# A gated mix of linear attention and a squared-ReLU layer: the first key-value burst queued as one block, and the first w1 tile loaded in four pieces

## The chip, the cores and the metric

The kernel runs on one core of one Trainium2 chip. The metric is the device time of one execution in microseconds (us); of several executions of one kernel the median counts.

## What is computed

The token matrix `x` (2048 x 512) goes through two branches, and a gate of one number per token mixes them. The input `B_x` is not used; both branches read `A_x`.

```python
g = sigmoid((x * gate_w).sum(-1, keepdims=True))
# branch a: 32 heads of 16, feature map with two softmaxes, linear attention
q, k, v = split(x @ wqkv)
phi(t)  = concat(softmax(t @ w_phi), softmax(-(t @ w_phi)))      # per head, 16 -> 32
kv, z   = phi(k)^T @ v, sum over tokens of phi(k)
a       = ((phi(q) @ kv) / (phi(q) . z + 1e-6)) @ wo
# branch b: dense layer of width 1792
h       = relu(x @ w1 + b1) ** 2
b       = h @ w2 + b2
out     = g * a + (1 - g) * b
```

## The kernel before, in words

**The dense layer paces everything.** The tokens are cut into 4 blocks of 512, the 1792 hidden columns into 14 tiles of 128. Two sweeps go over the 4 blocks, the first with hidden tiles 0 to 6, the second with 7 to 13, which makes 56 steps `t`. A step has an *up* product (`up`, tile `u`: 12 matmuls of 128 x 512) for step `t + 2` and the *down* products (`down`, tiles `d`: 4 token chunks of 3 matmuls each) for step `t`. Every fp32 product is written as three products of high and low parts (`mm3`, lines 73 to 77: high by high, line 75; high by low, line 76 or 77; low by high). The parts come from `split` (lines 65 to 71): ScalarE copies the high part (line 67), VectorE subtracts it to get the low part (line 70). `hidden` makes ReLU (line 455), square (456) and the split into `hh` and `hl`, which have three buffers each.

**The attention's work is laid between the steps.** Half of each step is a *slot*; `at(slot, f)` puts a function into a slot, and the loop at line 753 runs the functions of slot `2t`, the up product, the functions of slot `2t + 1`, then the down products. Keys and values are computed by pairs of token chunks with seven block products instead of eight (functions `p1` to `p7`, PSUM tiles `kx`, `ky`, `kz`); `features` turns a key chunk into exponentials, `normed` scales them, `values` writes a value chunk into `vext`. `do_kv(p)` then multiplies the features of pair `p` with its values: 64 matmuls of 32 columns (two chunks of 32, line 374), which all add into one PSUM tile `kvps` and which VectorE adds to `kvs` (line 612). This is the *key-value burst*; there are 8, one for each pair. Pair 1 begins at slot 13.5, so the first burst, of pair 0, is called in slot 17, ahead of the down products of step 8, together with `p7(1)` and `p3(1)`; `p4(1)` follows in slot 18. Slots 14, 16, 18 and 20 also load rows of `x` for the gate (`gate_load`, tile `in`), and two slots later VectorE multiplies and sums them (`gate_dot`, line 320).

**What sets the order.** The Tile scheduler orders each engine's instructions by priority and data. `tc.issue_after(i)` keeps what is written under it behind instruction `i` in the order; `tc.high_priority` pulls forward. After step 9's first two chunks of down products, `fold("q")` (line 202) builds a folded query weight: it fills two `u` tiles and both banks that `kx`, `ky` and `kz` use, and four VectorE transposes (line 224) empty them; the next up product and the next `kx` product need those banks again.

**The start.** `warm_up` runs 12 matmuls on constants. `start` (line 494) issues the four pieces of `x` on SP's queue (line 500), the first w1 tile on ScalarE's queue (line 501), then on SP two more w1 tiles and a w2 tile (`fetch`, line 109), then others. The first up product multiplies the raw fp32 pieces (line 518, for k = 0 to 3, each using columns `k * 128` to `k * 128 + 127` of the w1 tile). The next one (lines 469 and 471) needs the split parts of all four `x` pieces and of the second w1 tile; its first 128 columns are copied on their own (line 526).

The transfers of the two queues (SP's and ScalarE's) take turns on eight completion semaphores, named DMAHW0 to DMAHW7 in the program: a transfer waits until the one that had its semaphore before has landed.

Of the kernel before, what the change touches and what calls it, by code (L numbers as in the profile page):

```python
# [16 lines left out]
P = 128  # L17
S, D, H, DH, F = 2048, 512, 32, 16, 1792
NK = D // P
# [8 lines left out]
NV = 2  # L28
# [9 lines left out]
def tile_gated_mix(ctx: ExitStack, tc: tile.TileContext, xT, xn, wqT, wkT, wphi, wv, wo, w1, b1, w2, b2, gw, out):  # L38
    nc = tc.nc
# [14 lines left out]
    st, up_w, down_w = {}, {}, {}  # L54
# [10 lines left out]
    def split(src, hi, lo, ehi, elo):  # L65
        if ehi is nc.scalar:
            i = nc.scalar.activation(hi, src, AF.Copy)  # L67
        else:
            i = ehi.tensor_copy(hi, src)
        st["low"] = elo.tensor_tensor(lo, src, hi.bitcast(F32), ALU.subtract)  # L70
        return i
# [22 lines left out]
    def ffn_tiles(nm, fc):  # L94
        if fc >= NFH + NSTR:
            return slots(("B21", "T1", "T4", "T3")[fc - NFH - NSTR], int(nm == "w2"), f"{nm}{fc}")
        return (fpool.tile([P, 512], F32R, tag=nm + "h", name=f"{nm}h{fc}"),
                fpool.tile([P, 512], F32R, tag=nm + "l", name=f"{nm}l{fc}"))
# [5 lines left out]
    def fetch(nm, fc, t=None):  # L104
        src = w1[fc] if nm == "w1" else w2[fc * P:(fc + 1) * P, :]
        if t is None:
            t = load(src)
        else:
            nc.sync.dma_start(t, src)
        raw[nm, fc] = t  # L110
# [15 lines left out]
    def ready(nm, fc, elo=nc.vector):  # L126
        hi, lo = ffn_tiles(nm, fc)
        i = split(raw.pop((nm, fc)), hi, lo, nc.scalar, elo)
        (up_w if nm == "w1" else down_w)[fc] = hi, lo
        return i  # L130

    def ready_later(nm, fc, *elo):
        with tc.issue_after(st["act"].ins):
            ready(nm, fc, *elo)

    def x_tiles(b, k):
        return (xpool.tile([P, SB], F32R, tag="xh", name=f"xh{b}_{k}"),
                xpool.tile([P, SB], F32R, tag="xl", name=f"xl{b}_{k}"))
# [49 lines left out]
    vext = [hold.tile([P, H * VW + 32 - VW], F32, tag="vz", name=f"vext{i}") for i in range(NV)]  # L188
# [8 lines left out]
    def load_fold(nm, wT, tiles):  # L197
        st["wT", nm] = tiles
        for g in range(NK):
            nc.sync.dma_start(tiles[g], wT[:, g, :])  # L200
# [169 lines left out]
    def kv_chunk(n, kvps, phi, v):  # L370
        for i in range(NG):
            for j in range(4):
                h = 8 * (i % 4) + 4 * (i // 4) + j
                nc.tensor.matmul(kvps[32 * j:32 * j + 32, 32 * i:32 * i + 32], v[:, h * VW:h * VW + 32],  # L374
                                 phi[:, 32 * h:32 * h + 32],
                                 start=(n % 2 == 0 and i == 0), stop=(n % 2 == 1),
                                 skip_group_check=True)
# [75 lines left out]
    def hidden(fc, ps):  # L453
        r = work.tile([P, SB], F32, tag="r", name="r")
        nc.scalar.activation(r, ps, AF.Relu, bias=b1c[:, fc:fc + 1])  # L455
        nc.scalar.activation(r, r, AF.Square)  # L456
        hh = work.tile([P, SB], F32R, tag="hh", name="hh", bufs=LAG + 1)
        hl = work.tile([P, SB], F32R, tag="hl", name="hl", bufs=LAG + 1)
        st["act"] = split(r, hh, hl, nc.scalar, nc.vector)
        return hh, hl  # L460
# [33 lines left out]
    def start():  # L494
        w = work.tile([P, 2, 4, NG, 32], F32, tag="phiT", name="win", bufs=1).rearrange("p u r g s -> p (u r g s)")
        t = st["xr", 0] = [work.tile([P, 2 * D], F32, tag="tb", name="xin", bufs=2) for _ in range(2)]
        raw["w1", 0] = w[:, :D]
        xs = [t[k // 2][:, k % 2 * D:(k % 2 + 1) * D] for k in range(NK)]
        for k in range(NK):
            nc.sync.dma_start(xs[k], xT[0, :, k, :])  # L500
        nc.scalar.dma_start(w[:, :D], w1[0])
        fetch("w1", 1, w[:, D:2 * D])
        fetch("w1", 2, w[:, 2 * D:3 * D])
        fetch("w2", 0, w[:, 3 * D:])
        fetch("w1", 3)
        fetch("w2", 1)
        t = [wpool.tile([P, 512], F32, tag=tag, name="fold") for tag in ("T40h", "T30h", "T30l", "T31h", "T31l")]
        st["wphi"] = t[0]
        nc.sync.dma_start(t[0], wphi)
        load_fold("k", wkT, t[1:])  # L510
        fetch("w1", 4)
        fetch("w2", 2)
        ps = ps_u.tile([P, SB], F32, tag="u", name="u")
        st["x", 0] = []
        for k in range(NK):
            kk = slice(k * P, (k + 1) * P)
            with tc.issue_after(st["up"].ins):
                st["up"] = nc.tensor.matmul(ps, raw["w1", 0][:, kk], xs[k], start=k == 0, stop=k == NK - 1)
            hi, lo = x_tiles(0, k)
            split(xs[k], hi, lo, nc.scalar, nc.vector)  # L520
            st["x", 0].append((hi, lo))

        t = raw.pop(("w1", 1))
        hi, lo = up_w[1] = ffn_tiles("w1", 1)
        for j in (slice(0, P), slice(P, 512)):
            nc.scalar.activation(hi[:, j], t[:, j], AF.Copy)
        nc.vector.tensor_tensor(lo, t, hi.bitcast(F32), ALU.subtract)
        i = ready("w1", 2)
        with tc.issue_after(i.ins):
            hid[0] = hidden(0, ps)  # L530
        ready_later("w2", 0)
        with tc.issue_after(st["up"].ins):
            do_up(1)
        raw.pop(("w1", 0))
        fetch_v()
# [70 lines left out]

    def do_kv(p):
        ps = ps_u.tile([P, 2 * P], F32, tag="u", name="kvps")
        for m in (2 * p, 2 * p + 1):
            kv_chunk(m, ps, st["phi", m], vext[m % NV])  # L610
        with tc.high_priority(offset=AHEAD):
            nc.vector.tensor_tensor(kvs, kvs, ps, ALU.add)

# [48 lines left out]
    def at(slot, f, *a):  # L662
        steps.setdefault(int(slot), []).append(lambda: f(*a))
# [9 lines left out]
    for t in range(NB * NFH):  # L673
        for nm, s in (("w1", 2 * t - 8), ("w2", 2 * t - 4)):
            late = (nm, t % NFH) in KEPT_LATE
# [18 lines left out]
    at(20, foldq_move)  # L694
    starts = (8, 13.5, 20, 25.2, 30.4, 35.6, 40.8, 46)
    for p, s in enumerate(starts):
        todo = [(p1, s, p), (p6, s + 1, p), (p2, s + 1, p), (p5, s + 3, p)]
        if p:
            todo.append((do_kv, s + 3 + (p == 1), p - 1))
        todo += [(p7, s + 3 + (p == 1), p), (p3, s + 4, p), (p4, s + 5, p)]  # L700
        for f, slot, q in todo:
            at(slot, f, q)
    at(NB * SL - 2, do_kv, NPAIR - 1)
    for b in range(NB):
        for c in range(NC):
            s = b * SL + 2 * c if b else 7 + c
# [21 lines left out]
    for p in range(NB * NC // 2):  # L728
        n, s = 2 * p, 54 + 6 * p + 2 * (p > 0)
        q, late = divmod(n, NC)[0], p == NB * NC // 2 - 1  # L730
# [13 lines left out]
    def do_up(t):  # L744
        if t < len(work_list):
            sw, b, i = work_list[t]
            fc = sw * NFH + i
            hid[t] = up(fc, st["x", sw * NB + b], up_w[fc])
# [112 lines left out]
```

## Time and profile before

| | us |
|---|---|
| runs before, median of 3 (lowest, highest) | 510.41 (509.11, 511.47) |
| the profiled execution's own time | 508.94 |
| its span, from first to last instruction | 507.2 |
| matmul busy time on TensorE (PE) in the span | 503.0 |
| VectorE (DVE) / ScalarE (ACT) / GpSimd (POOL) busy | 404.0 / 254.2 / 75.0 |
| granted TensorE clock, mean | 0.999 of full |

A row of a timeline gives start, duration, engine, source line, operation, output and inputs, shape and count; in brackets stands how long the engine was idle before it and what ended that. Rows that repeat are merged, with the count behind the x. SPq and ACTq are the queues that issue transfers; PEld is the weight load that goes ahead of a matmul. A fp32 pass of a matmul counts as one instruction, and a 32-column matmul of the burst has two passes, so that a burst of 64 shows 128. A matmul's duration in a row is longer than its pitch, since matmuls overlap: what the next one waits is read from start to start.

### The profile page before, as it was taken

Reading aid. Unit: us, or ns where it says so; the run is one execution under the profiler, and the core shown is the slowest. Engines: PE = TensorE matmul, PEld = TensorE weight load, DVE = VectorE, ACT = ScalarE, POOL = GpSimd, SP = SyncE. Lnnn points to the kernel's source line nnn. Section 1 sums busy time; section 2 is a strip of 40 time slices with the busy share of each in tenths; the row PEclk is TensorE's granted clock in tenths of the full one; section 3 lists DMA queues with packets and bytes.
Section 4 is the critical chain, followed back from the end, with each engine's and each line's share of the span. In section 5 each row is a group of like instructions: output and inputs, shape, how many; then the busy total and the mean of one; then the engine's idle time right before and its main releaser. Section 6 shows DMA issues by size and latency. Waiting matters only on the chain.

```text
span 507.2 us, 9515 instructions
## 1 busy us (share of the span) xinstructions
PE 503.0 (99%) x3616; PEld 403.9 (80%) x3616; DVE 404.0 (80%) x642; ACT 254.2 (50%) x433; POOL 75.0 (15%) x77
## 2 busy tenths in 40 slices
PE   9999999999999999999999999999999999999997
PEld 4878877788888888888888878788787878788876
DVE  4979997867878777787889998978789676798724
ACT  6598571654654557273664744343525353433530
POOL 5303020202050000000004131202121212102100
PEclk9999999999999999999999999999999999999999
DMA  8899787984567656835658252213152221032102
GB/s 295 316 351 321 226 278 249 312 305 153 176 200 236 238 172 209 291 118 174 186 162 308 72 192 53 90 51 95 38 183 95 82 80 45 7 101 81 41 23 83
DMA packets 52437, 84.79 MB, mean 167 GB/s; under 512 B 8104, under 2 KB 14504, under 8 KB 52392
## 3 DMA queue, kind: packets, MB, share of 16 engines
q1 hardware_dynamic: 52072, 83.79, 51.1%
q8 instruction: 28, 0.46, 0.4%
q10 hardware_dynamic: 288, 0.39, 0.2%
q14 instruction: 17, 0.14, 0.1%
q0 software_dynamic: 32, 0.01, 0.0%
HBM read 56.37 MB, written 21.50 MB: 154 GB/s over the span
## 4 chain that ended last, share of the span: by engine, by line
PE 98%; ACT 1%; DVE 0%; issue 0%
PE d L75 10%; PE u L75 10%; PE d L77 10%; PE d L76 10%; PE u L76 10%; PE u L77 9%; PE q L75 3%; PE q L76 3%; PE q L77 3%; PE att L76 3%; PE att L77 3%; PE att L75 3%; PE ky L75 2%; PE ky L77 2%; PE ky L76 2%; PE kvps L374 2%
## 5 line engine op out<-in xcount | busy, mean ns | idle before, releaser
L455 ACT ACTIVATE r<-u,b1c 128x512 f32<-128x512 f32 x56 | 38.4, 686 | 148.8 <-PE u L77 148.8
L383 POOL TENSOR_TENSOR ez<-e,z 128x512 f32<-128x512 f32 x32 | 41.7, 1325 | 277.9 <-ACT e L354 160.5
L75 PE MATMUL d<-w2h,hh 128*128 128x512 f32 x160 | 63.1, 394 | 0.0
L77 PE MATMUL d<-w2h,hl 128*128 128x512 f32 x160 | 62.3, 390 | 0.0
L76 PE MATMUL d<-w2l,hh 128*128 128x512 f32 x160 | 62.3, 389 | 0.0
L75 PE MATMUL u<-xh,w1h 128*128 128x512 f32 x152 | 59.7, 393 | 0.1
L76 PE MATMUL u<-xl,w1h 128*128 128x512 f32 x152 | 59.2, 389 | 0.0
L77 PE MATMUL u<-xh,w1l 128*128 128x512 f32 x152 | 59.2, 389 | 0.0
L359 DVE TENSOR_REDUCE sm<-e 128x64 f32<-128x1024 f32 x32 | 38.9, 1214 | 20.3 <-ACT e L354 20.3
L70 DVE TENSOR_TENSOR hl<-r,hh 128x512 fp32r<-128x512 f32 x56 | 38.0, 678 | 16.0 <-ACT hh L67 16.0
L407 ACT ACTIVATE phiT<-tb 32x256 f32<-32x256 f32 x64 | 26.5, 413 | 32.1 <-DVE tb L401 31.5
L354 ACT ACTIVATE e<-e 128x1024 f32<-128x1024 f32 x32 | 33.8, 1055 | 12.6 <-DVE e L352 12.3
L67 ACT ACTIVATE hh<-r 128x512 fp32r<-128x512 f32 x56 | 35.3, 630 | 2.3 <-PE d L76 0.8
L456 ACT ACTIVATE r<-r 128x512 f32<-128x512 f32 x56 | 35.2, 629 | 1.3
L75 PEld LDWEIGHTS d<-w2h,hh 128*128 128x128 f32 x160 | 30.0, 188 | 6.5 <-issue 0.4
L272 POOL TENSOR_TENSOR row<-xin 128x256 f32<-128x256 f32 x16 | 17.8, 1120 | 117.4 <-DVE S4ol L70 27.6
L77 PEld LDWEIGHTS d<-w2h,hl 128*128 128x128 f32 x160 | 30.0, 188 | 6.3
L76 PEld LDWEIGHTS d<-w2l,hh 128*128 128x128 f32 x160 | 30.0, 188 | 6.0
L75 PEld LDWEIGHTS u<-xh,w1h 128*128 128x128 f32 x152 | 28.5, 188 | 7.9 <-issue 0.8
L77 PEld LDWEIGHTS u<-xh,w1l 128*128 128x128 f32 x152 | 28.5, 188 | 6.1
L76 PEld LDWEIGHTS u<-xl,w1h 128*128 128x128 f32 x152 | 28.5, 188 | 5.8
L385 DVE TENSOR_REDUCE dz<-ez 128x64 f32<-128x1024 f32 x16 | 19.4, 1210 | 9.4 <-POOL ez L383 9.3
(544 smaller groups left out, 1161.5 us busy)
## 6 DMA issues: line engine op xcount, KB each, us to landing
in<-in_w SPq DMA_DIRECT2D x66, 256.0 KB, 3.2
phiT<-tb SPq DMA_DIRECT2D x192, 32.0 KB, 1.9
w2l<-lkept SPq DMA_DIRECT2D x20, 256.0 KB, 4.0
w1l<-lkept SPq DMA_DIRECT2D x19, 256.0 KB, 3.5
xin<-in_xT SPq DMA_DIRECT2D x16, 256.0 KB, 5.7
xkept<-xh SPq DMA_DIRECT2D x16, 256.0 KB, 3.7
xkept<-xl SPq DMA_DIRECT2D x16, 256.0 KB, 4.2
in<-in_xn SPq DMA_DIRECT2D x16, 256.0 KB, 2.9
```

What stands on the lines that cost most here:

```text
L67: i = nc.scalar.activation(hi, src, AF.Copy)
L70: st["low"] = elo.tensor_tensor(lo, src, hi.bitcast(F32), ALU.subtract)
L75: nc.tensor.matmul(o, ah[:, sa], bh[:, sb], start=first, stop=False, **kw)
L76: nc.tensor.matmul(o, ah[:, sa], bl[:, sb], start=False, stop=False, **kw)
L77: return nc.tensor.matmul(o, al[:, sa], bh[:, sb], start=False, stop=last, **kw)
L354: nc.scalar.activation(ef, ef, AF.Exp)
L359: nc.vector.tensor_reduce(sm, e3, AX.X, ALU.add)
L383: nc.gpsimd.tensor_tensor(ez[:, hs, :], e3[:, hs, :], zbc[half], ALU.mult)
L385: nc.vector.tensor_reduce(dz, ez, AX.X, ALU.add)
L407: nc.scalar.activation(dst, src, AF.Copy)
L455: nc.scalar.activation(r, ps, AF.Relu, bias=b1c[:, fc:fc + 1])
L456: nc.scalar.activation(r, r, AF.Square)
```

## The change

In `do_kv`, the 64 matmuls stand under `tc.issue_after(st["down"].ins)`, that is, behind the last down product written so far. The first burst, `p7(1)` and `p3(1)` move from slot 17 to slot 18 (`late`). The first w1 tile is loaded on ScalarE's queue in four transfers of 128 columns (64 KB each, 512 bytes in each of 128 partitions) instead of one of 512 columns (256 KB, 2 KB in each).

```diff
-        nc.scalar.dma_start(w[:, :D], w1[0])
+        for k in range(NK):
+            kk = slice(k * P, (k + 1) * P)
+            nc.scalar.dma_start(w[:, kk], w1[0, :, kk])
...
     def do_kv(p):
         ps = ps_u.tile([P, 2 * P], F32, tag="u", name="kvps")
-        for m in (2 * p, 2 * p + 1):
-            kv_chunk(m, ps, st["phi", m], vext[m % NV])
+        with tc.issue_after(st["down"].ins):
+            for m in (2 * p, 2 * p + 1):
+                kv_chunk(m, ps, st["phi", m], vext[m % NV])
...
     for p, s in enumerate(starts):
+        late = 1.5 * (p == 1)
         todo = [(p1, s, p), (p6, s + 1, p), (p2, s + 1, p), (p5, s + 3, p)]
         if p:
-            todo.append((do_kv, s + 3 + (p == 1), p - 1))
-        todo += [(p7, s + 3 + (p == 1), p), (p3, s + 4, p), (p4, s + 5, p)]
+            todo.append((do_kv, s + 3 + late, p - 1))
+        todo += [(p7, s + 3 + late, p), (p3, s + 4 + late / 2, p), (p4, s + 5, p)]
```

On TensorE the order changes only around the first burst; the other seven bursts already stood as whole blocks and stay where they are. Before, right behind the up product of step 10, the burst's first matmuls stand between the down products of step 7 (`d_960` to `d_963` are its four chunks), and the other 58 follow behind them, ahead of `ky`, `kz` and the down products of step 8:

```order
L76 MATMUL u<-xl_3_606,w1h_780 128x512
L77 MATMUL u<-xh_3_605,w1l_781 128x512
L374 MATMUL kvps<-e,vext_114 32x32 x2
L75 MATMUL d_960<-w2h_768,hh 128x512
L76 MATMUL d_960<-w2l_769,hh 128x512
L77 MATMUL d_960<-w2h_768,hl 128x512
L374 MATMUL kvps<-e,vext_114 32x32 x2
L75 MATMUL d_961<-w2h_768,hh 128x512
L76 MATMUL d_961<-w2l_769,hh 128x512
L77 MATMUL d_961<-w2h_768,hl 128x512
L374 MATMUL kvps<-e,vext_114 32x32
L75 MATMUL d_962<-w2h_768,hh 128x512
```

Now the down products of steps 7 and 8 stand in one piece behind the up product (one `ky` matmul ahead of them), and this is the end of step 8's (`d_966`, its last chunk), where the burst follows as one block and the rest of `ky` and `kz` behind it:

```order
L75 MATMUL d_966<-w2h_777,hh 128x512
L76 MATMUL d_966<-w2l_778,hh 128x512
L77 MATMUL d_966<-w2h_777,hl 128x512
L374 MATMUL kvps<-e,vext_114 32x32 x32
L374 MATMUL kvps<-e,vext_115 32x32 x32
L76 MATMUL ky<-T30l,S_731 128x512
L77 MATMUL ky<-T30h,S_731 128x512
L75 MATMUL ky<-T31h,S_731 128x512
L76 MATMUL ky<-T31l,S_731 128x512
L77 MATMUL ky<-T31h,S_731 128x512
```

The burst has moved behind 24 down matmuls, and the five places where TensorE went to 32-column matmuls and back have become one. On VectorE, at the same place in the program (`hl` are low parts of the hidden tile, `in,lg` is the gate's product and sum, `vext` the values of pair 1, `k` the keys of its second chunk), the order was:

```order
L70 TENSOR_TENSOR hl<-r,hh 128x512
L612 TENSOR_TENSOR kvs<-kvs,kvps 128x256
L361 RECIPROCAL r<-sm 128x64
L320 SCALAR_TENSOR_TENSOR in,lg<-in,gwb 128x512
L365 TENSOR_TENSOR e<-e,r 128x1024
L564 TENSOR_TENSOR vext_115<-ky,t_1005 128x32x16
L564 TENSOR_TENSOR vext_114<-kz,t_900 128x32x16
L70 TENSOR_TENSOR hl<-r,hh 128x512
L320 SCALAR_TENSOR_TENSOR in,lg<-in,gwb 128x512
L564 TENSOR_TENSOR k_1149<-ky,t_847 128x512
L349 TENSOR_REDUCE mx<-k_1149 128x32
```

and is now:

```order
L70 TENSOR_TENSOR hl<-r,hh 128x512
L361 RECIPROCAL r<-sm 128x64
L320 SCALAR_TENSOR_TENSOR in,lg<-in,gwb 128x512
L365 TENSOR_TENSOR e<-e,r 128x1024
L70 TENSOR_TENSOR hl<-r,hh 128x512
L615 TENSOR_TENSOR kvs<-kvs,kvps 128x256
L566 TENSOR_TENSOR vext_115<-ky,t_1008 128x32x16
L320 SCALAR_TENSOR_TENSOR in,lg<-in,gwb 128x512
L566 TENSOR_TENSOR vext_114<-kz,t_903 128x32x16
L566 TENSOR_TENSOR k_1152<-ky,t_850 128x512
L349 TENSOR_REDUCE mx<-k_1152 128x32
```

The addition to `kvs` has moved behind the second `hl`, and the `vext` write from `kz` behind the second gate product. On SP's queue at the start (the waits in brackets are the completion semaphores), before:

```order
L500 DMA xin<-in_xT 128x512 x4
L109 DMA win<-in_w 128x512 x3
L85 DMA in<-in_w 128x512 [waits DMAHW0_49]
L85 DMA in<-in_w 128x512 [waits DMAHW1_49]
L509 DMA fold<-in_wphi 128x512 [waits DMAHW2_49]
L200 DMA fold<-in_wkT 128x512 [waits DMAHW3_49]
```

and now:

```order
L500 DMA xin<-in_xT 128x512 x4
L109 DMA win<-in_w 128x512 [waits DMAHW0_49]
L109 DMA win<-in_w 128x512 [waits DMAHW1_49]
L109 DMA win<-in_w 128x512 [waits DMAHW2_49]
L85 DMA in<-in_w 128x512 [waits DMAHW3_49]
L85 DMA in<-in_w 128x512 [waits DMAHW4_49]
L511 DMA fold<-in_wphi 128x512 [waits DMAHW5_49]
```

The four pieces of `x` and the four pieces of the first w1 tile now hold all eight semaphores, so that SP's fifth transfer, the second w1 tile, waits for the first piece of `x` to land; before, the first wait was in its eighth transfer. On ScalarE only the four transfers in place of one are new, and nothing moves on GpSimd.

## The prediction

> **What bounds the kernel now.** I read the page's busy times and its chain of waits first, then the timeline of TensorE around the first burst, at the fold that follows it, and at the start.
>
> ```profile
> PE 503.0 (99%) x3616; PEld 403.9 (80%) x3616; DVE 404.0 (80%) x642; ACT 254.2 (50%) x433; POOL 75.0 (15%) x77
> PE 98%; ACT 1%; DVE 0%; issue 0%
> ```
>
> TensorE is busy for 503.0 of 507.2 us, and 98% of the chain that ended last is TensorE. So time is won only where TensorE itself does less or waits less, and it is lost wherever TensorE is made to wait. The profiled execution took 508.94 us; the median of the runs is 510.41, 1.47 more. I work against the first and add the sum to both. About 0.5% (2.5 us) is what a measurement of this kernel can tell from no change; that is the bound of "faster" and "slower" below.
>
> **The burst: what it removes.** In the timeline of TensorE, each row with its start:
>
> ```profile
> 72.89 0.39 PE L77 MATMUL u<-xh,w1l 128*128 128x512 f32 x1
> 73.20 0.26 PE L374 MATMUL kvps<-e,vext 128*32 128x32 f32 x4
> ...
> 76.94 0.39 PE L76 MATMUL d<-w2l,hh 128*128 128x512 f32 x1
> ...
> 77.50 1.20 PE L374 MATMUL kvps<-e,vext 128*32 128x32 f32 x116
> ...
> 78.96 0.40 PE L76 MATMUL ky<-T30l,S 128*128 128x512 f32 x1
> ...
> 84.19 0.39 PE L75 MATMUL ky<-T40h,xh 128*128 128x512 f32 x1
> ...
> 106.91 0.39 PE L77 MATMUL kz<-T11h,S2ol 128*128 128x512 f32 x1
> 107.23 1.30 PE L374 MATMUL kvps<-e,vext 128*32 128x32 f32 x128
> ...
> 108.79 0.40 PE L76 MATMUL ky<-T30l,S2oh 128*128 128x512 f32 x1
> ```
>
> The pitch of an ordinary matmul comes from 78.96 to 84.19: 23 matmuls in 5.23 us, 0.227 us each. From 72.89 to 78.96 stand 14 ordinary matmuls (the last of the up product, 12 down, one `ky`), 14 x 0.227 = 3.18 us. The other 2.89 us went to the first burst and its five visits to 32-column matmuls. The second burst stands in one piece: from 106.91 to 108.79 are 1.88 us, less two matmuls (0.45) leaves 1.43. One piece instead of five saves 2.89 - 1.43 = **1.46 us** of TensorE's own time. No instruction is added or removed.
>
> Moved products could wait for data, but I find no such wait. The four chunks of step 7 need their banks emptied by VectorE, and the first would now start at about 73.35, the fourth at 75.39; these evacuations (line 806) stand back to back from 72.17 to 74.89, each half a microsecond ahead. If that cover went, the lost time would come off the 1.46.
>
> **The burst: what is late next.** TensorE reaches the fold 1.46 us earlier, and there it already waits for VectorE:
>
> ```profile
> 92.36 2.50 DVE L224 STREAM_TRANSPOSE wqin<-foldq 128x512 f32<-128x512 f32 x4
> ...
> 92.81 0.40 PE L77 MATMUL d<-w2h,hl 128*128 128x512 f32 x1
> ...
> 94.31 0.50 PE L75 MATMUL kx<-B110h,xh 128*128 128x512 f32 x1
> 94.65 0.40 PE L76 MATMUL kx<-B110l,xh 128*128 128x512 f32 x1
> ```
>
> From 92.81 to 94.65 are six pitches, 1.36 us, but 1.84 passed: TensorE lost 0.48 us, because `kx` needs the bank that the third of the four transposes empties (92.36 plus three quarters of 2.50 is 94.24). So there is no slack: whatever of the 1.46 us the transposes don't also move is lost again here. What the transposes wait for, in the order of time on SP's queue, VectorE and ScalarE:
>
> ```profile
> 77.37 0.32 SPq L118 DMA_DIRECT2D w2l<-lkept  x1
> ...
> 79.65 0.42 SPq L85 DMA_DIRECT2D in<-in_xn  x1
> ```
>
> ```profile
> 81.86 0.68 DVE L564 TENSOR_TENSOR vext<-kz,t 128x512 f32<-128x512 f32 x1
> 82.45 0.68 DVE L70 TENSOR_TENSOR hl<-r,hh 128x512 fp32r<-128x512 f32 x1
> 85.63 0.69 DVE L320 SCALAR_TENSOR_TENSOR in<-in,gwb 128x512 f32<-128x512 f32 x1 [2.49 <-DMA in<-in_xn]
> 86.24 0.08 DVE L320 DVE_READ_ACCUMULATOR in<-in,gwb 128x1 f32 x1
> 86.24 0.68 DVE L564 TENSOR_TENSOR k<-ky,t 128x512 f32<-128x512 f32 x1
> ...
> 91.75 0.69 DVE L70 TENSOR_TENSOR hl<-r,hh 128x512 fp32r<-128x512 f32 x1 [2.31 <-ACT hh L67]
> ```
>
> ```profile
> 89.47 1.06 ACT L354 ACTIVATE e<-e 128x1024 f32<-128x1024 f32 x1 [0.32 <-DVE e L352]
> ...
> 91.08 0.63 ACT L67 ACTIVATE hh<-r 128x512 fp32r<-128x512 f32 x1
> ```
>
> Backwards: the transposes follow `hl` (91.75), which waits for ScalarE's `hh` (91.08), which stands behind the exponential (89.47), which waits for VectorE's feature steps, which begin with `k<-ky` at 86.24, which stands behind the gate product, and that waited 2.49 us for its row of `x` (`in_xn`). So the chain hangs on a transfer, not on TensorE.
>
> Two things move it. Earlier: `in_xn` is issued behind `w2l<-lkept`, whose buffer is released by step 7's last `w2l` matmul, begun at 76.94 and over at 77.33. In the new order that matmul is the 12th behind 72.89 (`ky`, then 11 down matmuls), so it starts at 72.89 + 12 x 0.227 = 75.62, 1.32 us earlier, and SP's whole queue behind it follows. Later: the `vext` write from `kz` now stands between the gate product and `k<-ky`, and costs 0.59 us there (81.86 to 82.45). I take both: the chain and the transposes come 1.32 - 0.59 = 0.73 us earlier, and 1.46 - 0.73 = 0.73 us goes back into the wait for the transposes. The burst's term is **-0.7 us**. It ends at -1.46 if the chain moves in full, and at +0.6 if the row of `x` lands no earlier than before, since TensorE then waits for transposes that are 0.59 later.
>
> The addition to `kvs` and the `vext` write from `ky` come 2.1 and 0.4 us later, I estimate; the next `ky` matmul that reuses the bank comes at 84.19 - 1.46 = 82.73, behind the write's end at about 82.3. That cover is thin; without it the stall would be what it lacks.
>
> **The start: what it adds.** Rows of ScalarE, SP and TensorE:
>
> ```profile
> 0.74 0.41 ACTq L501 DMA_DIRECT2D win<-in_w  x1
> ...
> 2.59 1.61 SPq L109 DMA_DIRECT2D win<-in_w  x3
> 5.20 0.82 SPq L85 DMA_DIRECT2D in<-in_w  x2
> ...
> 7.97 0.63 ACT L67 ACTIVATE xh<-xin 128x512 fp32r<-128x512 f32 x1 [0.69 <-DMA xin<-in_xT]
> 8.67 0.72 ACT L526 ACTIVATE w1h<-win 128x128 fp32r<-128x128 f32 x2
> 9.04 0.50 PE L469 MATMUL u<-xh,w1h 128*128 128x512 f32 x1
> 7.99 0.30 PEld L518 LDWEIGHTS u<-xin,win 128*128 128x128 f32 x2 [0.75 <-DMA xin<-in_xT]
> ```
>
> ```profile
> DMA to landing us min/median/max: 6.1/6.1/6.1
> DMA to landing us min/median/max: 2.1/2.1/2.1
> 0.00:5.00 5.00, 4.22 (x11) 1.56 (x12) 0.00 (x0) 1.28 (x1) 2.13 (x13) 1.00 0.49 158
> ```
>
> The last row is the window from 0 to 5 us, with its mean of 158 GB/s at the end; the two above it are the landing times of line 109's transfers and of three `part<-row` transfers (line 811) on a quiet queue. The path is the last piece of `x` (landed at 7.97), ScalarE's copy of it, its copy of the second w1 tile's first columns (8.67), and TensorE's first use (9.04). The first w1 tile isn't on this path: its four pieces can only bring the first matmul forward, which then waits for `x`. Three extra issues of 0.41 us stand ahead of ScalarE's first copy and end at 0.74 + 4 x 0.41 = 2.4, long before there is anything to copy.
>
> What does change is the second w1 tile. It was issued at 2.59; now it waits until the first piece of `x` has landed, as the transfers at 5.20 do in this trace. At about 5.1 then, 0.79 MB (5 us at 158 GB/s) of the 1.31 MB ahead of it are moved, and 0.52 MB at the 350 GB/s of the next fence take 1.5 us. With 2.1 us for a transfer on a quiet queue it lands at 8.7. The small packets add to that:
>
> ```profile
> DMA packets 194, 0.35 MB, mean 350 GB/s; under 512 B 23, under 2 KB 23, under 8 KB 194
> ...
> q1 hardware_dynamic: 194, 0.35, 98.7%
> ```
>
> ```profile
> DMA packets 385, 0.27 MB, mean 54 GB/s; under 512 B 128, under 2 KB 384, under 8 KB 384
> ...
> q1 hardware_dynamic: 384, 0.26, 20.1%
> ```
>
> The first is 6 to 7 us (171 packets of 2 KB), the second 280 to 285 us (256 of 1 KB). With 20 ns assumed for the smallest (a guess of mine that matters little), a 2 KB packet takes (15.8 - 0.5) / 171 = 0.090 us and one of 1 KB (16.1 - 2.6) / 256 = 0.053, so 512 bytes, which no row shows, come to 0.034 along that line: 32 for each of 16 engines instead of 8 large ones are 1.10 instead of 0.72 us, 0.4 more, about half of it ahead of the tile. That makes 8.9 against 8.67 now. The start's term is **+0.3 us**. Its ends: -0.55, if `x` lands so much sooner that TensorE's idle of 0.75 shrinks to the usual 0.2; and +2.5, if the second tile takes 6.1 us from 5.1, as it took from 2.59.
>
> A rule of the Trainium skill speaks against this part: the page "DMA: Bandwidth & Descriptors", section "Rules for kernel authors", says to coalesce many small transfers, since "under 64 KB you're paying mostly overhead", and each piece is 64 KB. Its table of measured bandwidth (section "Bandwidth") gives 0.95 us for 64 KB; four in a row would take 3.8 us where the row above gives 0.72, an estimate of +3.1 us, and the sum would be +2.4. The packets of this trace don't bear that out; their price is the rival below.
>
> **Sum.** -0.7 + 0.3 = -0.4 us: 508.94 becomes 508.5, and the median 510.41 becomes **510.0 us**.
>
> **The rivals.**
>
> - *The burst's gain arrives in full* (-1.46, start +0.3: 509.2). For it: TensorE is the bound everywhere else. Against it: the 0.48 us already lost at the fold. It needs the row of `x` to land 2 us earlier. Chance 0.2; with the start's best end it reaches 508.4.
> - *The second w1 tile is late*, and this makes the kernel slower. It happens at the start: with the tile issued at 5.1 and landing in 5.0 us instead of 3.6, the first use is 1.5 us late, and with the burst's -0.7 the time is 511.2; at 6.1 us it is 512.2. It decides from a first copy later than 8.67 + 0.7 = 9.4. For it: every transfer issued near 5.2 in this trace was in a full queue. Against it: half as many bytes are now queued ahead. Chance 0.2.
> - *The row of `x` keeps its time*, so the inserted `vext` write only delays the transposes: +0.6 + 0.3, 511.3. For it: its landing at 85.6 also depends on other transfers. Against it: its place behind the released buffer. Chance 0.08.
> - *Small packets cost more than the line gives.* If 512 bytes take as long as 1 KB, 32 x 0.053 = 1.70 us instead of 0.72, the start is +1.0: 510.7. Chance 0.05.
>
> **How the numbers follow.** My forecast (within half a microsecond of 510.0) has 0.47. The range takes in the best rival's 508.4 and the late tile's 512.2. Faster by over 0.5% would need -2.55 us, more than both best ends together (-2.0), so only the scatter of the runs (2.4 us) gives it 0.08; slower by as much needs the late tile at its worst end and a burst that gains nothing: 0.06. Within 0.5%: 0.86.
>
> **What would show it.** Right: one `kvps` row of 128 passes behind 24 down matmuls; a larger gap ahead of `kx` at the fold, near 1.2 instead of 0.48 us; the gate product's wait ending near 84.3; `k<-ky` about 0.7 earlier. At the start the second w1 tile issued at the landing of the first `x` piece, and TensorE's line 469 near 9.3. Wrong: `kx` without a gap, a gate product still at 85.6, line 469 at 8.6 or beyond 10.

## The result, and the profile after

The changed kernel took 509.64 us in the median of 12 runs (508.41 to 512.99), the kernel before 509.83 beside it (509.09 to 511.47, 12 runs): a ratio of 1.0001, 95% interval 0.998 to 1.0022. That is no change, and the forecast of 510.0 is 0.4 us off. But the number came out by other steps than those written down: one term was lost for a reason that the prediction had only as a rival, and one loss was not in it at all, so that the close number is luck. The changed kernel's runs also scatter over 4.6 us, those of before over 2.4. That is the first sign of the loss.

The profiled execution took 508.97 us, with a span of 507.2 again. Its busy times and its chain of waits:

```profile
PE 501.7 (99%) x3616; PEld 404.5 (80%) x3616; DVE 402.9 (79%) x642; ACT 254.5 (50%) x433; POOL 73.6 (15%) x77
PE 93%; ACT 3%; DVE 1%; DMA 1%; issue 0%; SPq 0%; DVEq 0%
```

TensorE is busy for 1.3 us less (503.0 before), and the span is the same: what it no longer does, it waits. The chain says the same, with 7% on other engines where it was 2%. TensorE at the burst and at the fold, the timeline's rows with start, duration, engine, line and tiles:

```profile
73.28 0.39 PE L77 MATMUL u<-xh,w1l 128*128 128x512 f32 x1
...
78.94 0.39 PE L77 MATMUL d<-w2h,hl 128*128 128x512 f32 x1
79.26 1.30 PE L374 MATMUL kvps<-e,vext 128*32 128x32 f32 x128
...
91.77 0.40 PE L77 MATMUL d<-w2h,hl 128*128 128x512 f32 x1
93.20 0.50 PE L75 MATMUL u<-xh,w1h 128*128 128x512 f32 x1 [1.04 <-DVE wqin L224]
...
94.74 0.39 PE L76 MATMUL kx<-B110l,xh 128*128 128x512 f32 x1
```

I measure two stretches here and in every run below. **The first** goes from the last up product ahead of the burst (73.28) to the last down product ahead of the fold (91.77): 18.49 us, against 19.92 before (72.89 to 92.81). The burst in one piece saves 1.43 us. **The second** goes from there to the second `kx` product (94.74): 2.97 us, against 1.84. Of the 1.43 us, 1.13 are gone again. The chain that the transposes hang on, from SP's queue and VectorE:

```profile
76.42 0.32 SPq L118 DMA_DIRECT2D w2l<-lkept  x1
...
78.69 0.47 SPq L85 DMA_DIRECT2D in<-in_xn  x1
```

```profile
85.11 0.69 DVE L320 SCALAR_TENSOR_TENSOR in<-in,gwb 128x512 f32<-128x512 f32 x1 [2.47 <-DMA part<-row]
...
85.73 0.69 DVE L566 TENSOR_TENSOR vext<-kz,t 128x512 f32<-128x512 f32 x1
86.33 0.68 DVE L566 TENSOR_TENSOR k<-ky,t 128x512 f32<-128x512 f32 x1
...
92.44 2.50 DVE L224 STREAM_TRANSPOSE wqin<-foldq 128x512 f32<-128x512 f32 x4
```

The row's transfer is issued 0.96 us earlier than before (79.65), but its product begins only 0.52 earlier (85.63), and the inserted `vext` write takes all of that: `k<-ky` and the transposes stand 0.08 to 0.09 us later than before. The bracket names `part<-row`, the transfer issued right behind the row; it is inferred, and the row's own landing is put at 6.3 us behind its issue, 85.0, where it took 5.8 us before. At the start, the rows of ScalarE, SP and TensorE:

```profile
7.25 0.63 ACT L67 ACTIVATE xh<-xin 128x512 fp32r<-128x512 f32 x1 [0.35 <-DMA xin<-in_xT]
7.90 0.72 ACT L528 ACTIVATE w1h<-win 128x128 fp32r<-128x128 f32 x2
```

```profile
4.67 1.28 SPq L109 DMA_DIRECT2D win<-in_w  x3
```

```profile
0.78 5.28 PE L491 MATMUL warm<-const-bfloat16-1.0 128*128 128x512 bf16 x12 [0.78 <-PEq L854]
5.85 4.02 PE L520 MATMUL u<-xin,win 128*128 128x512 f32 x8
9.30 0.79 PE L469 MATMUL u<-xh,w1h 128*128 128x512 f32 x1
...
12.47 0.39 PE L75 MATMUL u<-xh,w1h 128*128 128x512 f32 x1
```

The second w1 tile is issued late, as forecast (4.67, not 2.59), but it and the last piece of `x` are there 0.7 to 0.8 us earlier than before (copies at 7.90 and 7.25, not 8.67 and 7.97). Further executions below show that this is scatter for the most part. TensorE is late all the same: line 75 begins at 12.47, not 11.88. It waits for nothing at 5.85; its 12 warm-up products took 5.28 us instead of 4.67. Whether that comes from the change, one profile cannot say.

### The profile page after: what moved, and what is told of

It reads as the page before. It is cut to its first block, busy times and chain, and to the rows that moved or that the text cites. A ratio compares the mean times of both kernels' runs of the same rounds, so it can differ in the third digit from the quotient of the medians.

```text
span 507.2 us, 9522 instructions
## 1 busy us (share of the span) xinstructions
PE 501.7 (99%) x3616; PEld 404.5 (80%) x3616; DVE 402.9 (79%) x642; ACT 254.5 (50%) x433; POOL 73.6 (15%) x77
## 4 chain that ended last, share of the span: by engine, by line
PE 93%; ACT 3%; DVE 1%; DMA 1%; issue 0%; SPq 0%; DVEq 0%
PE u L75 10%; PE d L75 9%; PE d L77 9%; PE d L76 9%; PE u L77 9%; PE u L76 9%; PE q L75 3%; PE q L76 3%; PE q L77 3%; PE att L76 3%; PE att L75 3%; PE att L77 3%; PE ky L75 2%; PE ky L77 2%; PE ky L76 2%; PE kvps L374 2%
## 5 line engine op out<-in xcount | busy, mean ns | idle before, releaser
L359 DVE TENSOR_REDUCE sm<-e 128x64 f32<-128x1024 f32 x32 | 38.8, 1214 | 20.3 <-ACT e L354 20.3
```

What stands on the lines that cost most here:

```text
L359: nc.vector.tensor_reduce(sm, e3, AX.X, ALU.add)
```

## The experiments

The theory to test: the burst saves its 1.4 us, and loses it at the fold because the transposes hang on the transfer of the row of `x`, whose landing does not follow its issue. The rivals: the loss came from the shifted start, or the transposes hang on something else. "Line 75" below is its first row, the end of the start.

### Each part alone

The first kernel is the change without the four transfers, the second the four transfers without the rest.

> The burst's part of the change alone; the first w1 tile comes in one transfer, as before. Two stretches of TensorE tell: from the last up product ahead of the burst (72.89 before, 73.28 after) to the last down product ahead of the fold (92.81, 91.77), 19.92 us before and 18.49 after; and from there to the second kx product (94.65, 94.74), 1.84 before and 2.97 after. Theory (the saved 1.4 us is mostly lost again in the wait for the transposes, whose chain hangs on the row of x): 18.5 and 3.0 here as well, sum 21.5 against 21.8 before, so 0.3 us less time; VectorE's gate product still waits about 2.5 us for its row. Rival (the 1.1 us given back at the fold came from the later start of the changed kernel's profiled execution, which shifted TensorE against the transfers): with the old start the second stretch is 2.2 to 2.6, the sum 20.7 to 21.1, and the time 0.7 to 1.1 us less.

> The start's part alone: four transfers of 128 columns, the burst as before. Theory (the start of the changed kernel was late because its 12 warm-up products all ran at 0.43 us, which is chance of the execution, and not because of the transfers): the copies of x and of the second w1 tile end early as in the changed kernel (last copy of x at 7.2, first w1h at 7.9, against 7.97 and 8.67 before), and the first use at line 469 follows the end of the warm-up products: near 9.3 to 9.7 if they end at 5.85 again, 8.6 to 9.0 if they end at 5.3 or sooner. The first row of line 75 stands at 11.9 or less in the second case, 12.5 in the first. Rival (the split itself delays TensorE, by its small packets or its extra semaphores): line 75 at 12.4 or later whenever the warm-up products end. Stretches at the burst 19.9 and 1.8, as before. Time within 0.6 us of before either way.

The burst alone: 509.02 us against 509.44 (ratio 1.0, 0.9985 to 1.0015). Its rows on SP's queue, VectorE and TensorE:

```profile
78.38 0.42 SPq L85 DMA_DIRECT2D in<-in_xn  x1
```

```profile
85.49 0.69 DVE L320 SCALAR_TENSOR_TENSOR in<-in,gwb 128x512 f32<-128x512 f32 x1 [3.17 <-DMA in<-in_xn]
```

```profile
93.59 0.50 PE L75 MATMUL u<-xh,w1h 128*128 128x512 f32 x1 [1.77 <-DVE wqin L224]
...
95.12 0.39 PE L76 MATMUL kx<-B110l,xh 128*128 128x512 f32 x1
```

The stretches are 18.46 and 3.70, together 22.16 us: in this execution the burst cost 0.4 us more than before (21.76). The start was 0.3 us earlier than in the changed kernel's profile and the loss larger, so the shifted start was not the reason. The loss is also larger than the theory's (3.70 us in the second stretch where 3.0 was expected, a sum of 22.16 where 21.5 was). The medians are 0.4 us apart, inside their interval. The row's transfer was issued 1.27 us earlier than before and its product began 0.14 earlier.

The split alone: 509.51 against 509.44 (1.0001, 0.9993 to 1.001), stretches 19.93 and 2.03. Line 75 is at 11.70, with warm-up products that ended at 5.68 instead of 6.06: between the theory's two cases, at the second one's line 75. The copies were not as early as the theory had them: the last of `x` at 7.71, not 7.2, and the first `w1h` at 8.37, not 7.9. And TensorE's weight loads show a wait that I had ruled out:

```profile
6.02 0.19 PEld L520 LDWEIGHTS u<-xin,win 128*128 128x128 f32 x1 [0.31 <-DMA win<-in_w]
...
6.96 0.47 PEld L520 LDWEIGHTS u<-xin,win 128*128 128x128 f32 x2 [0.39 <-DMA win<-in_w]
7.91 0.38 PEld L520 LDWEIGHTS u<-xin,win 128*128 128x128 f32 x2 [0.48 <-DMA win<-in_w]
8.73 0.19 PEld L469 LDWEIGHTS u<-xh,w1h 128*128 128x128 f32 x1 [0.45 <-ACT w1h L528]
```

It waits for each further piece of the first w1 tile (`win`), which lands beside its piece of `x`, the last at 7.9. Before, the whole tile was there at 5.2, as this row shows, and TensorE waited for the last piece of `x` at 7.99:

```profile
5.23 0.30 PEld L518 LDWEIGHTS u<-xin,win 128*128 128x128 f32 x2 [0.27 <-DMA win<-in_w]
```

One wait has taken the other's place. What released line 469 is the same in both: ScalarE's copy of the second w1 tile (8.73 here, 9.04 before), which stands behind the last copy of `x`.

### The row's product out of the way

On the burst alone, and on the kernel before:

```diff
-        with tc.issue_after(st["low"].ins):
+        with tc.issue_after(st["feat" if n == NC + 1 else "low"].ins):
...
-            nc.vector.tensor_tensor(e[:, :, 1, :], bc(mn), pv, ALU.subtract)
+            st["feat"] = nc.vector.tensor_tensor(e[:, :, 1, :], bc(mn), pv, ALU.subtract)
```

> The burst's part, and the gate product of the row that waited for its transfer (line 320, row 5) is issued behind the feature steps of the second chunk of pair 1, not ahead of them, so that k<-ky no longer stands behind the transfer. Theory (the transposes hang on that transfer): the wait of about 2.5 us ahead of the gate product goes from this place, k<-ky begins near 84.7 instead of 86.3, the transposes near 90.9 instead of 92.4, the stretch from the last down product to the second kx product shrinks from 2.97 to 1.4 to 1.7 us, and nearly the whole 1.4 us of the burst arrives: about 1.1 us less than the burst alone. Rival (the transposes hang on ScalarE's exponential and the copies behind it, or on the ky product itself, and the gate product only stood in a wait that was there anyway): k<-ky gains less than 0.4 us and the second stretch stays at 2.6 to 3.0.

> The kernel before, with only the gate product of row 5 moved behind the feature steps. Theory (this takes away the 0.48 us lost at the fold of the kernel before, and the burst's 1.4 us come on top of it only with the change): the stretch from the last down product to the second kx product is 1.4 us instead of 1.84, the one ahead of it 19.9 as before, and the time 0.3 to 0.6 us less than before. Rival (the gate product's place is worth its 1.5 us by itself, whatever the burst does): 1.2 us less or more. No run below a mean clock of 0.998 by either.

With the burst: 508.38 us against 509.44 (0.9985, 0.997 to 0.9999). VectorE and TensorE:

```profile
84.61 0.69 DVE L564 TENSOR_TENSOR k<-ky,t 128x512 f32<-128x512 f32 x1 [0.67 <-PE ky L77]
...
90.78 2.50 DVE L224 STREAM_TRANSPOSE wqin<-foldq 128x512 f32<-128x512 f32 x4
```

```profile
91.67 0.39 PE L77 MATMUL d<-w2h,hl 128*128 128x512 f32 x1
...
93.08 0.39 PE L76 MATMUL kx<-B110l,xh 128*128 128x512 f32 x1
```

`k<-ky` now waits for TensorE's own product, the transposes come at 90.78, and the second stretch is 1.41 us. Both stretches make 19.89 us, 1.87 less than before. The theory's numbers in the profile are met and the rival falls: the transposes hung on that transfer. In the medians the gain over the burst alone is 0.64 us (509.02 to 508.38), not the 1.1 expected.

On the kernel before: 508.75 against 509.55 (0.9985, 0.9976 to 0.9994), with stretches of 19.94 and 1.41. The profile shows the 0.43 us that were expected. The median shows 0.8, a little over the 0.3 to 0.6, with an interval of 0.3 to 1.2. Beside it, the burst with the moved product is 1.46 us shorter over the two stretches (19.89 against 21.35), but both stand at 0.9985 of the kernel before: that the burst's saving comes on top is shown by one profile of each, and not by the medians.

### The clock at the fold

The changed kernel's 12 runs had a mean granted clock of 0.999 or 1.000 in seven (508.41 to 510.2 us) and of 0.995 to 0.997 in five (510.88 to 512.99). Unchanged, it was run twice more.

> The changed kernel once more, to see how much two executions of it differ. Five of its 12 runs had a mean granted clock of 0.995 to 0.997 and took 510.9 to 513.0 us, the other seven 508.4 to 510.2; none of 29 runs of the kernel before was below 0.999. Theory A (the clock falls at the fold, where TensorE now stands idle for 1.0 to 1.8 us ahead of the u and kx products): if this profile shows such an execution, the granted clock is near 0.5 for some 3 us behind 93 us, and near 1.00 in the first 20. Theory B (it falls at the start, as in the version with pieces of 32 rows, where the granted clock was 0.65 and 0.50 in the stretches 8 to 10 and 10 to 12 us behind an idle time of 2.4 us): the low stretch lies between 6 and 14 us, and the fold looks as before. If this execution is at full clock: span 506.5 to 508.5, line 75's first row at 11.7 to 12.5, and the gap between the last down product and the second kx product 2.6 to 3.8 us, with VectorE's gate product landing anywhere between 85.0 and 85.6 whenever its transfer was issued.

> As the run before it, the changed kernel unchanged; a second execution raises the chance that one of the two shows the low clock. Theory A: granted clock near 0.5 for some 3 us behind the fold at 93 us. Theory B: near 0.5 for some 3 us between 6 and 14 us. At full clock: as in the run before, span 506.5 to 508.5.

They took 510.27 (1.0019, 1.0002 to 1.0036) and 510.43 us (1.0016, 1.0 to 1.0031) against 509.32, and both profiles caught the lower clock. TensorE's product behind the wait, and the windows (busy time of each engine; the third number from the end is the granted clock) of the first:

```profile
93.33 0.51 PE L75 MATMUL u<-xh,w1h 128*128 128x512 f32 x1 [1.53 <-DVE wqin L224]
```

```profile
92.00:94.00 2.00, 0.67 (x3) 0.59 (x4) 2.00 (x4) 1.30 (x3) 1.92 (x3) 1.00 1.07 382
94.00:96.00 2.00, 2.00 (x7) 1.28 (x6) 2.00 (x3) 0.66 (x2) 0.00 (x0) 0.68 0.79 251
96.00:98.00 2.00, 2.00 (x7) 1.52 (x6) 2.00 (x6) 0.60 (x1) 0.00 (x0) 0.50 1.10 318
98.00:100.00 2.00, 2.00 (x10) 1.65 (x9) 1.51 (x2) 0.37 (x1) 0.00 (x0) 0.97 0.88 279
```

and of the second:

```profile
93.89 0.80 PE L75 MATMUL u<-xh,w1h 128*128 128x512 f32 x1 [2.55 <-DVE wqin L224]
```

```profile
92.00:94.00 2.00, 0.10 (x1) 0.11 (x1) 2.00 (x3) 1.61 (x4) 1.80 (x2) 0.94 0.99 361
94.00:96.00 2.00, 2.00 (x5) 1.61 (x6) 2.00 (x4) 0.53 (x2) 0.00 (x0) 0.50 0.83 272
96.00:98.00 2.00, 2.00 (x7) 1.57 (x7) 2.00 (x5) 0.00 (x0) 0.00 (x0) 0.71 0.99 305
```

Theory A holds: the clock falls to half at the fold, and is 1.00 in the first 20 us. What is missing to 1.00 adds up to 3.4 us at half clock in each: in the first (0.32 + 0.50 + 0.03) x 2 us / 0.5. That is 1.7 us of TensorE's work. The second stretches are 3.56 and 5.24 us, the latter with the clock already down. The clock is down from 94.7 to 98.1 us in the first, beginning 1.4 us behind the end of the wait, and from 93.8 in the second, as the wait ends; while TensorE still has work, it falls in no other stretch of either execution. The row's transfer was issued at 78.33 and 77.88, up to 1.8 us earlier than before, and its product began at 85.07 and 85.26.

Over its three series the changed kernel has 18 runs of 32 at full clock (median 509.0) and 14 below (511.5), 510.2 in all. None of the 108 runs of the kernel before beside the experiments is below 0.998, nor any of the 22 of the split alone and of the moved product on the kernel before; 2 of 12 of the burst alone are. Where the clock fell is seen in two of the 14; of the other twelve only the mean is known. The Trainium skill has this fall on the page "TensorE: Matmul & The Clock Gate": the section "What's actually happening" gives a free-running window of 3413 ns, and the 3.4 us here agree. Its section "Why this matters for your kernels" allows idle gaps up to about 3 us, and that is not what these runs show: falls came with waits of 1.5 and 2.6 us in two executions, while 1.8 us with the burst alone and 2.2 us in one below left the clock at 1.00.

### The start: another split, and less warm-up

The kernel before with the first w1 tile in four pieces of 32 rows, and the changed kernel with 8 warm-up products:

```diff
-        nc.scalar.dma_start(w[:, :D], w1[0])
+        for k in range(NK):
+            kk = slice(k * 32, (k + 1) * 32)
+            nc.scalar.dma_start(w[kk, :D], w1[0, kk, :])
```

```diff
-        for _ in range(12):
+        for _ in range(8):
```

> Kernel before with the first w1 tile in four transfers too, but of 32 rows each, so that each packet keeps its 2 KB and only the number of transfers (and of completion semaphores) is that of the change. Theory (x and the second w1 tile came 0.7 us sooner in the changed kernel because the second w1 tile was held back until a semaphore was free, and left the queues to x): the transfers of line 109 are issued at 4.5 to 5.1 instead of 2.59, and the last copy of x stands at 7.2 or sooner. Rival (x came sooner because the first w1 tile in small packets takes its share of the queues more slowly): the issue is late here too, but the last copy of x stands at 7.8 to 8.0 as before. Line 469 follows the later of the warm-up products' end plus 3.5 us and the last copy's end. Time within 0.6 us of before.

> The changed kernel with 8 warm-up products instead of 12; they end at 4.2 us instead of 5.5 to 6.1. Theory (in the changed kernel's profile the start hung on TensorE's own slow passes, not on the transfers: the first piece of x was there at 4.5, the last at 7.2, and the four passes ran without a wait from 5.85 on): the passes start at about 5.0, wait for each piece, and line 469 begins near 8.4 to 8.7, line 75 near 11.3 to 11.7 instead of 12.47; 0.8 to 1.1 us less time than the changed kernel's profile. Rival (with less warm-up TensorE is still slow when the products come, or falls back while it waits for the pieces): passes at 0.85 us instead of 0.43, line 75 at 12.5 to 14, and more runs with a mean clock below 0.998.

The pieces of rows: 512.44 against 509.44 (1.0052, 1.0037 to 1.0067, four runs, of which two are below 0.998). The transfers of line 109 are issued late (4.44), and the last copy of `x` stands at 7.95 as before. So holding the second w1 tile back does not by itself make `x` come sooner. Nor is the rival shown, since what both explain lies inside the scatter: over the eight executions with the split in columns the last copy of `x` stands at 7.25 to 8.23, and of the five with one transfer two have it at 7.97 and 8.15 and three at about 7.4 to 7.6. The result I had not expected by either, and the windows behind it, of TensorE and its weight loads:

```profile
8.05 5.37 PE L520 MATMUL u<-xin,win 128*128 128x512 f32 x8 [2.37 <-DMA win<-in_w]
```

```profile
9.37 0.34 PEld L520 LDWEIGHTS u<-xin,win 128*128 128x128 f32 x1 [0.52 <-issue]
10.22 0.34 PEld L520 LDWEIGHTS u<-xin,win 128*128 128x128 f32 x1 [0.52 <-issue]
```

```profile
8.00:10.00 2.00, 1.95 (x3) 0.93 (x4) 1.82 (x3) 1.92 (x4) 1.91 (x2) 0.65 1.04 385
10.00:12.00 2.00, 2.00 (x4) 0.75 (x3) 1.83 (x2) 0.01 (x1) 2.00 (x3) 0.50 1.09 367
```

The first product now needs all four pieces, and begins at 8.05. The clock falls right behind this wait (0.50 from 8.6 to 12.0 us), the passes run 0.85 us apart, and line 75 begins at 15.99, 4.1 us late.

With 8 warm-up products the rival holds: 511.15 against 509.32 (1.0034, 1.0014 to 1.0054). The passes begin at 4.96, the earliest so far, but run 0.85 us apart until 9.4; line 75 is at 13.58. The last four products of the warm-up are not spare: TensorE is still slow without them. At the fold it waited 2.21 us at a clock of 1.00; four of its 12 runs are below 0.998.

### What is late next

Three versions of the changed kernel with the row's product moved: with 8 warm-up products, with 12, and with 12 and the fourth store of the first batch's part rows issued beside the other three. The last kernel is that with the first w1 tile in one transfer.

```diff
-                at(2 * t + 3 + c // 2, lambda *a: nc.sync.dma_start(*a), dst, o)
+                at(2 * t + 3 + (c // 4 if b == 0 else c // 2), lambda *a: nc.sync.dma_start(*a), dst, o)
```

> The changed kernel with both corrections: the gate product behind the feature steps, and 8 warm-up products. If both theories hold the parts add: the gate product's place gave 1.6 us at the fold with the burst alone (kx at 93.08 instead of 95.12 with starts 0.02 us apart, less 0.2 us each for the row's scatter), the shorter warm-up up to 1.0: 506.5 to 507.5 us in the median against 509.4 of the kernel before. If the warm-up costs what it saves: 508.0 to 508.6. If the clock falls in more of the runs: 509 or more.

> The changed kernel with the gate product of row 5 behind the feature steps, and with its 12 warm-up products. Theory (the changed kernel loses at the fold twice: by the wait for the transposes, and in some executions by a clock that falls to half while TensorE stands idle there, as the granted clock of 0.50 to 0.68 at 94 to 98 us in both repeated executions shows): with the wait gone, no or nearly no run below a mean clock of 0.998 (14 of 32 of the changed kernel were), and 507.3 to 508.2 us in the median, at or below that of the version with 8 warm-up products (508.12), whose start was late by 0.7 to 1.5 us. Rival (the low clock comes with the burst in one piece or with the faster pace, not with the idle time at the fold): a third or more of the runs are low, and the median is 508.5 to 509.5.

> The changed kernel with the gate product moved, and the fourth store of the first batch's part rows issued with the other three (near 75 us, not 79.2), so that the fourth slab of the query fold, whose buffer it frees, is issued with the other three slabs near 78 instead of 86.3. Theory (with the gate product out of the way, the next wait at the fold is TensorE's for that slab: 0.34 to 0.63 us in the two versions that show it, with a pause of 1.3 to 1.5 us behind it in which TensorE waits for nothing that the profile shows): the 128 fold products stand in one row of 1.9 us without a wait, the stretch from the last up product ahead of the burst to the second kx product is 19.8 to 20.0 us (21.70 with the gate product alone moved, 21.76 before), no run is below a mean clock of 0.998, and the median is 507.3 to 508.2. Rival 1 (the pause is not caused by the slab, but by the fetching of TensorE's instructions, which no order of transfers here takes away): the slab's wait is gone and a pause of 1.3 to 1.5 us still stands near 92; median 508.3 to 509.0. Rival 2 (the weight load that now stands behind the four stores comes late and holds up ScalarE): TensorE waits before 88 us, median 509 or more.

> As the run before it, but with the first w1 tile in one transfer. Theory (the four transfers at the start neither gain nor lose: 0.07 us in the median alone): the same median within 0.4 us, and the same fold. Rival (the pause near 92 us, seen in both versions with the four transfers and the gate product moved and not in the one without them, depends on the three instructions that the four transfers add): no pause here, one in the run before it, and 1 us or more between the medians.

| kernel | median us (before) | ratio, 95% interval | line 75 | stretches, us | below 0.998 |
|---|---|---|---|---|---|
| 8 warm-up products | 508.12 (509.32) | 0.9977, 0.9966 to 0.9989 | 13.18 | 20.21 + 1.39 | 0 of 12 |
| 12 warm-up products | 508.80 (509.55) | 0.9992, 0.9979 to 1.0005 | 12.19 | 20.34 + 1.36 | 1 of 11 |
| and store earlier | 509.02 (509.61) | 0.9992, 0.9982 to 1.0003 | 12.20 | 19.14 + 1.36 | 1 of 11 |
| and one transfer | 508.06 (509.61) | 0.9980, 0.9967 to 0.9992 | 11.62 | 20.17 + 1.37 | 1 of 12 |

The second stretch is 1.4 us in all four. With the wait gone the lower clock nearly goes: 5 of 58 runs, with the first kernel of the kind above, against 20 of the 56 that have the burst without the moved product. The closest pair, the burst alone and with the product moved, has 2 of 12 each, so that the link rests on the changed kernel's series. But the medians of the first three lie above the first theory's ranges; that of 8 warm-up products falls under "costs what it saves", and of 12 into its rival's range, with a clock that speaks for the theory. The first stretch has grown from 18.5 to between 19.1 and 20.3. The fold products and their weight loads in the last kernel:

```profile
87.84 1.87 PE L209 MATMUL foldq<-row,in 32*32 32x128 f32 x125
91.03 0.40 PE L209 MATMUL foldq<-row,in 32*32 32x128 f32 x3 [1.32 <-issue]
```

```profile
q8 instruction: 1, 0.02, 12.8%
```

The fourth slab of the fold is there in time, its wait is gone, and a pause still stands before the last three of 128 products (the last four in two others, right behind them in the first), in which TensorE waits for nothing that the profile shows: rival 1. TensorE's products stand still for up to 1.3 us here, and the clock stays at 1.00. The second fence is the queue of instructions in the window 88.5 to 89.0, one packet of 0.02 MB. In the four executions that packet starts at 90.7, 89.7, 88.0 and 88.5, and TensorE goes on at 92.94, 92.07, 90.60 and 91.03, always 2.2 to 2.6 us behind. In the first kernel with the product moved it starts at 87.2, so that products would go on at 89.4 to 89.8, ahead of the place at 90.2 to 90.4 where they would stop, and there is no pause. In all ten executions without the pause such a packet starts 1.2 to 3.1 us ahead of the fold products, in the four with it between 0.4 us ahead and 1.3 behind. That TensorE waits for its own instructions is thus well supported, though not shown by taking the packet away, which wasn't tried; why the packet is late in these four stays open. The Trainium skill's page "Runtime: NRT & Kernel Launch", section "Instruction fetch mechanics", tells of refills in blocks of 16 KiB whose cost is "mostly hidden"; the size agrees with the packet, and the pauses of 0.6 to 1.6 us, at mean DMA shares of 0.61 to 1.05 in the windows from 88 to 92, are, if the link holds, what it leaves out. The store's place helped by nothing that the medians show. The split's rival is refuted in its main part: the pause is there with one transfer too. But the 1 us between the last two medians is more than expected; their line 75 is 0.58 us apart, the slower one has the shorter first stretch in its profile, and the rest is open. Open too is what a microsecond at the start is worth: the version with 8 warm-up products has line 75 1.0 us later than that with 12, and the lower median. The last kernel and the first are the fastest found, 1.2 to 1.6 us below the kernel before.

## Why the prediction was right, and where it was not

**The burst's own saving** was forecast at 1.46 us, and measured at 1.43, 1.46, 1.44 and 1.44 in four executions with the changed burst alone or in the changed kernel. That part was right by its mechanism. The four chunks of step 7 and `ky` had their banks in time, as forecast.

**What is given back** was the step that failed: "SP's whole queue behind it follows". The queue did follow: `w2l` was issued 0.95 us earlier at a start 0.39 later, so 1.34 in place of 1.32. But I took the landing to move with the issue. Over six executions the transfer is issued between 77.88 and 79.65, 1.77 us apart, and the product behind it begins between 85.07 and 85.70, 0.63 apart; from issue to landing it took 5.8 us before and 6.3 to 7.3 with the earlier issue. With 8 warm-up products it was issued at 79.79, and the product began at 87.33. What else sets the landing stays open. So the row comes 0.1 to 0.6 us earlier, not 1.32; the `vext` write's 0.59 us was right; and the transposes came 0.1 to 0.8 us later rather than 0.73 earlier (in the last of them 0.5 us is a longer `hl`, 1.23 us instead of 0.69). The gap ahead of `kx` is 1.61 us in the changed kernel's profile, 2.97 less six pitches, and not near 1.2. The burst's term was -0.3 and +0.4 us in the two profiles at full clock, not -0.7. The rival with a chance of 0.08, a row that keeps its time, described this best.

**The clock at the fold** was in no step. I priced the wait by its length alone. Where the clock falls, it costs another 1.7 us; this is shown in two executions, and 14 of 32 have a mean that fits a fall.

**The start** was forecast at +0.3 us through a second w1 tile that lands at 8.9 us. It was issued near when I said (4.67 for 5.1), but was there by 7.9 in the changed kernel's profile. The sentence that the first w1 tile "isn't on this path" held only in part: TensorE waited for its last piece at 7.9 in the split alone, but ScalarE's copy still released line 469. That line 469 stood at 9.30, as forecast, is luck, since in that execution it followed from warm-up products that ended at 6.06. The term itself was rounded up, as 8.9 against 8.67 is 0.2, and the 20 ns in its price of a packet stands in no row. Line 75 begins at 11.65 to 12.47 in the six executions with the split and 12 warm-up products, mean 12.06, and at 11.62 to 12.18 in the five without, mean 11.91: +0.15 us, inside a scatter of 0.6 to 0.8 us in each group. Both the end of the warm-up products (4.97 to 6.06 us) and the last copy of `x` (7.25 to 8.23) go into it: the earliest end, 4.97, goes with a copy at 8.23 and line 75 at 12.20. So neither sign nor size of the term is shown, and the mechanism was not the one forecast. That many small packets cost much more was refuted here: the split alone is at 1.0001.

**The sum** fell at 509.6 because a larger give-back and the half clock, neither priced right, weighed against a kernel that at full clock is some 0.4 us faster than before (509.0 against 509.3 to 509.6 beside the experiments). The 32 runs together, at 510.2, are 0.4 to 0.9 us above before (509.3 to 509.8): within half a per cent, and inside the range. That two misses nearly cancelled is luck.

## What to carry to other kernels

When work on the bounding engine gets shorter, follow the chain that the next stage hangs on to its transfer, and bound the landing from both sides: an earlier issue into a full queue may bring nothing. Here one vector product that waited for a transfer stood ahead of work that didn't need it; moving that product was worth more than the change. And price a wait of TensorE of a microsecond and a half or more by the clock it may lose, not only by its length: a wider scatter of the runs with a lower mean clock is the sign to look for.

## What the runs showed that I had not expected

- Behind a wait of 1.5 us the clock can fall to half, for 3.4 us in all three executions that show a fall; a wait of 2.2 us at the same place left it alone. So the length alone does not decide; what else does is not shown.
- The granted clock reads 1.00 in the first 4 us of every profile, where the warm-up products stand 0.43 us apart, as the products at a granted 0.50 do. At the start the distance of products tells, not that column.
- Four transfers of 64 KB, issued within 2 us, landed over some 3 us, each beside a piece of `x`; one of 256 KB was there at 5.2 to 5.9 us. The pieces of 32 rows did no better than those of 128 columns, which speaks against the size of the packets as what held them.
- When one packet of instructions starts 1 to 3 us later, TensorE pauses for up to 1.6 us in the middle of a kernel; that it waits for this packet is inferred from the times.
